# Probabilities of a decode attention transposed 128 rows at a time, and the softmax denominators of both batches formed in one step

## The chip, the cores and the metric

The kernel runs on one core of one Trainium2 chip. The metric is the device time of one execution in microseconds (us); lower is better. A ratio is the mean time of one kernel's runs over the mean of the other's in the same rounds, so it isn't quite the ratio of the medians that stand beside it.

## The reference

One decode step: 2 batches, 1 query token each, 32 heads of 128, a cache of 4096 positions, a gated mix with a small ReLU network.

```python
B, Sq, D = 2, 1, 512
Hq, Hkv, Sk, Dh = 32, 32, 4096, 128
q = (x @ wq).reshape(B, Sq, Hq, Dh).transpose(0, 2, 1, 3)
scores = jnp.einsum("bhqd,bhkd->bhqk", q, k_cache) * (Dh ** -0.5)
p = softmax(scores, axis=-1)
o = jnp.einsum("bhqk,bhkd->bhqd", p, v_cache)
a = o.transpose(0, 2, 1, 3).reshape(B, Sq, Hq * Dh) @ wo
b = jnp.maximum(B_x @ w1, 0) @ w2
g = sigmoid((x * gate_w).sum(-1, keepdims=True))
return g * a + (1 - g) * b            # all inputs bfloat16
```

The two caches are 64 blocks of 2 MB (32 of keys, 32 of values; a block is two heads of one batch). Together with the weights 145.43 MB have to be read.

## The kernel before

The instruction streams of the engines are built in program order, with named events between them. One queue (SP) issues all large loads, in order, into a ring of four buffers. A load waits until the block that used its buffer before has been consumed.

```python
for n in range(64):                      # 32 key blocks, then 32 value blocks
    waits = []
    if n >= NSLOT:                       # NSLOT = 4
        prev = n - NSLOT
        waits.append(f"T_{prev}_7" if prev < 32 else f"pv_{prev - 32}")
    load(f"ld_kv_{n}", kv_sb[:, n % NSLOT, :, :], kv_in(n), waits=waits, ...)
WO_CUTS = (0, 16, 24, 28, 30, 32)        # the output projection's weights, 4 MB, come last
for k in range(5): ...
```

So the load of value block 4 waits for `pv_0`, the end of the first block's product of probabilities and values (PV block 0). Between the scores and PV stands the softmax, one batch `g` after the other. A row of `E_sb[g]` is one of 4 groups of positions times 32 heads.

```python
def ptrans(g):                           # 64 transposes of 32 rows x 64 columns per batch
    for q in range(4):
        for k in range(16):
            ...
            src = E_sb[g][32 * q:32 * q + 32, col0:col0 + 64]
            P.add("pe", ... e.transpose(bank16(2 * g + b, 32 * blk, 32, 0, 64), src,
                        ident16[32*q:32*q+32, 32*q:32*q+32], tile_position=(32 * q, 0)), ...)

def denom_l(g):   # VectorE: lm[g] = jmask * l4[g]; waits for the exp of batch g
def denom(g):     # PE: ones @ lm[g], for g = 1 only after rg_0; VectorE: rinv, then rg
def stage_p(i):   # VectorE: two copies, the probabilities of block i out of PSUM into pst
def PV(p):        # PE: 64 matmuls with 2 moving columns; block i >= 2 waits for oT of block i - 2

for g in range(2):
    row_max(g); exps(g); ptrans(g)
for i in (0, 2, 1, 3):
    stage_p(i)
for g in range(2):
    denom_l(g); denom(g)
P.begin_loop(NIT)                        # 8 passes of 4 PV blocks
```

(Cuts are marked with dots, and bodies not needed for the argument are told in a comment. `l4` holds the sums of the exponentials that the exp leaves behind, one per row; `lm` spreads them so that a matmul with `ones` adds the four groups of a head; `rinv` is the reciprocal of that denominator, and `rg` is `rinv` times the gate.) Each engine takes its instructions in order, so PE reaches PV block 0 only after both batches' transposes and both denominator matmuls.

Of the kernel before, what the change touches and what calls it, by code (L numbers as in the profile page):

```python
# [4 lines left out]
ALU = mybir.AluOpType  # L5
# [9 lines left out]
PER = 4  # L15
# [120 lines left out]
def bass_gated_mix__gqa_block_cached__dense_activation_relu__decode_kernel(  # L136
# [12 lines left out]
    P = _Prog(nc)  # L149
# [3 lines left out]
    ident16 = sb("ident16", [128, 128], b16)  # L153
# [3 lines left out]
    ones = sb("ones", [128, 128], f32)  # L157
# [5 lines left out]
    g_sb = sb("g_sb", [128, 2], f32)  # L163
# [7 lines left out]
    kv_sb = sb("kv_sb", [128, NSLOT, 64, 128], b16)  # L171
# [3 lines left out]
    E_sb = [sb(f"E{g}", [128, 1024], b16) for g in range(2)]  # L175
    pst = sb("pst", [128, PER, 64, 2], b16)
# [5 lines left out]
    lm = sb("lm", [128, 2, 32], f32)  # L182
    rinv = sb("rinv", [128, 2, 32], f32)
    rg = sb("rg", [128, 2, 32], f32)
# [7 lines left out]
    PSB = PSF[:, :].bitcast(b16)  # L192

    def bank(b, c0, n, p0=0, p1=128):
        return PSF[p0:p1, 512 * b + c0:512 * b + c0 + n]

    def bank16(b, c0, n, p0=0, p1=128):
        return PSB[p0:p1, 1024 * b + c0:1024 * b + c0 + n]
# [8 lines left out]
    MISC, ACC = 7, 6  # L207
# [4 lines left out]
    def o_col(p):  # L212
        return bank(4 + p % 2, 256 + 2 * p, 2)

    def p_place(r):

        c = r // 8
        q = c % 4
        return q % 2, ((q // 2) * 2 + c // 4) * 8 + r % 8

    x_in = A_x.rearrange("b s d -> (b s) d")
    gw_in = gate_w.rearrange("(o d) -> o d", o=1)
# [22 lines left out]
    for n in range(64):  # L245
        waits = []
# [5 lines left out]
    for k in range(5):  # L252
# [7 lines left out]
          waits=["c_i0"], signal="c_id")  # L260
    P.add("pool", lambda e: e.memset(qmask[:], 0.0), signal="c_qm")
    P.add("pool", lambda e: e.memset(jmask[:], 0.0), signal="c_j0")
    for q in range(4):
# [3 lines left out]
              waits=[f"c_j{q}"], signal=f"c_j{q + 1}")  # L267
# [3 lines left out]
    for q in range(4):  # L271
        P.add("pool", lambda e, q=q: e.memset(dmask[32 * q:32 * q + 32, q:q + 1], 1.0), waits=["c_d0"] if q == 0 else [],
              signal="c_d" if q == 3 else None)
# [4 lines left out]
    for g in range(2):  # L278
        for c in range(8):
            P.add("pe", lambda e, g=g, c=c: e.matmul(S_chunk(g, c), lhsT=zt[:, 0:32], rhs=zt[:, :], start=True, stop=True,  # L280
                                                     tile_position=(0, 32 * (c % 4)), skip_group_check=True),
                  waits=["c_zt"] if c + g == 0 else [])
    for t in range(4):
        P.add("pe", lambda e, t=t: e.transpose(bank16(4, 2 * t, 2), x_sb[0:2, t:512:4], ident16[0:2, 0:2]),
              waits=["c_id", "ld_x"] if t == 0 else [], signal="xT" if t == 3 else None)
    for t in range(4):
        P.add("pe", lambda e, t=t: e.transpose(bank16(5, 2 * t, 1), gw_sb[0:1, t:512:4], ident16[0:1, 0:1]),  # L287
              waits=["ld_gw"] if t == 0 else [], signal="gwT" if t == 3 else None)
    P.add("dve", lambda e: e.tensor_copy(out=xT_sb[:, :, :], in_=bank16(4, 0, 8).rearrange("p (t b) -> p t b", t=4)),
          waits=["xT"], signal="xT_sb")  # L290
    P.add("dve", lambda e: e.tensor_copy(out=gwb_sb[:, :, :],
                                         in_=PSB[:, 5120:5128:2].unsqueeze(2).to_broadcast([128, 4, 128])),
          waits=["gwT"], signal="gwb")
    for t in range(4):
        P.add("pe", lambda e, t=t: e.matmul(bank(6, 0, 2), lhsT=gwb_sb[:, t, :], rhs=xT_sb[:, t, :],
                                            start=(t == 0), stop=(t == 3)),
              waits=["xT_sb", "gwb"] if t == 0 else [], signal="logit" if t == 3 else None)
    P.add("act", lambda e: e.activation(out=g_sb[:, :], in_=bank(6, 0, 2), func=ACT.Sigmoid), waits=["logit"], signal="g")
    P.add("dve", lambda e: e.tensor_scalar(out=gm_sb[:, :], in0=g_sb[:, :], scalar1=-1.0, scalar2=1.0, op0=ALU.mult, op1=ALU.add),
          waits=["g"], signal="gm")  # L300
    for h in range(HQ):
        for t in range(4):
            P.add("pe", lambda e, h=h, t=t: e.matmul(bank(7, 2 * h, 2), lhsT=wq_sb[:, t, h * 128:(h + 1) * 128],  # L303
                                                     rhs=xT_sb[:, t, :], start=(t == 0), stop=(t == 3)),
                  waits=["ld_wq"] if h + t == 0 else [], signal="qT" if h == HQ - 1 and t == 3 else None)
# [83 lines left out]
              waits=[f"negM_{g}"], signal=f"E_{g}")  # L389

    def ptrans(g):
        for q in range(4):
            for k in range(16):
                c = q + 4 * (k // 8)
                r = 8 * c + k % 8
                b, blk = p_place(r)
                col0 = (c // 4) * 512 + (k % 8) * 64
                src = E_sb[g][32 * q:32 * q + 32, col0:col0 + 64]
                P.add("pe", lambda e, q=q, b=b, blk=blk, src=src: e.transpose(  # L399
                    bank16(2 * g + b, 32 * blk, 32, 0, 64), src, ident16[32 * q:32 * q + 32, 32 * q:32 * q + 32], tile_position=(32 * q, 0)),  # L400
                    waits=[] if k else [f"pt_{g}_{q - 2}" if q > 1 else f"E_{g}"], signal=f"pt_{g}_{q}" if k == 15 else None)

    def denom_l(g):
        P.add("dve", lambda e: e.tensor_scalar(out=lm[:, g, :], in0=jmask[:, :], scalar1=l4[:, g:g + 1], scalar2=None, op0=ALU.mult),
              waits=[f"E_{g}", "c_j4"], signal=f"lm_{g}")

    def denom(g):
        P.add("pe", lambda e: e.matmul(bank(MISC, 32 * g, 32), lhsT=ones[:, :], rhs=lm[:, g, :], start=True, stop=True),  # L408
              waits=[f"lm_{g}", "c_one"] + (["rg_0"] if g else []), signal=f"lb_{g}")
        P.add("dve", lambda e: e.reciprocal(out=rinv[:, g, :], in_=bank(MISC, 32 * g, 32)), waits=[f"lb_{g}"], signal=f"rinv_{g}")  # L410
        P.add("dve", lambda e: e.tensor_scalar(out=rg[:, g, :], in0=rinv[:, g, :], scalar1=g_sb[:, g:g + 1], scalar2=None, op0=ALU.mult),
              waits=[f"rinv_{g}", "g"], signal=f"rg_{g}")


    def stage_p(i):
        hp, g = divmod(i, 2)
        p = i % PER
        for hh in range(2):
            base = PSB[0:64, 2048 * g:2048 * g + 2048].rearrange("p (b k j) -> p b k j", b=2, k=32)
            P.add("dve", lambda e, hh=hh, base=base: e.tensor_copy(  # L420
                out=pst[64 * hh:64 * hh + 64, p, :, hh].rearrange("p (b k) -> p b k", b=2), in_=base[:, :, :, 2 * hp + hh]),
                waits=[f"pt_{g}_2", f"pt_{g}_3", "c_ps"] + ([f"pv_{i - PER}"] if i >= PER else []),
                signal=f"pst_{i}" if hh else None, sem=f"ps{p}")

    def o_norm(i):
        hp, g = divmod(i, 2)
# [3 lines left out]

    def PV(p):
        for r in range(64):
            b, blk = p_place(r)

            def waits(t):
                i = PER * t + p
                return [f"ld_kv_{32 + i}", f"pst_{i}"] + ([f"oT_{i - 2}"] if i >= 2 else [])
            P.add("pe", lambda e, iv, r=r, k=32 * b + blk: e.matmul(o_col(p), lhsT=kv_sb[:, p, r, :], rhs=pst[:, p, k, :],  # L438
                                                                    start=(r == 0), stop=(r == 63)),
                  waits=waits if r == 0 else [], signal=(lambda t: f"pv_{PER * t + p}") if r == 63 else None)  # L440

# [59 lines left out]
    for g in range(2):  # L501
        row_max(g)
        exps(g)
        ptrans(g)
    for i in (0, 2, 1, 3):
        stage_p(i)
    for g in range(2):
        denom_l(g)
        denom(g)
    P.begin_loop(NIT)  # L510
    for p in range(PER):
        PV(p)
    P.end_loop()
    for i in range(32):
        o_norm(i)
        if i + PER < 32:
            stage_p(i + PER)
# [3 lines left out]
          waits=["proj"], signal="res")  # L521
    for b, eng in enumerate(("sp", "act")):
        P.add(eng, lambda e, b=b: e.dma_start(out_ap[b].rearrange("(c n) -> c n", c=4), out_sb[b:97 + b:32, :]), waits=["res"],
              signal=f"st_{b}", sem="st", inc=16)
# [51 lines left out]
```

## Time and profile before

| | before |
|---|---|
| time, median of the six runs of both rounds before and after the prediction | 354.77 us (354.48 to 354.87) |
| span of the profiled execution | 352.9 us |
| read from HBM, rate over the span | 145.43 MB, 412 GB/s |
| PE busy, VectorE busy | 68%, 38% of the span |
| chain that ended last (followed back from the last instruction, each time to what released it) | PE 51%, DMA 44% |

The shares of busy time point at PE, but they average two halves with different limits. These are two lines of the profile's page: the granted TensorE clock in tenths, and the rate of transfers, each in 40 equal slices of the span.

```profile
PEclk9999999999999999999996555555555555555555
...
GB/s 342 400 417 431 423 425 427 430 425 433 426 423 431 428 431 427 431 427 423 431 427 424 204 438 423 438 420 436 425 431 426 425 433 423 435 423 427 431 420 160
```

The rate is flat at about 428 GB/s in both halves, whether PE is busy or not, with one exception: the 23rd slice (194.1 to 202.9 us) has 204. That is the only place, besides start and tail, where the load queue was not working. The clock line shows that it falls to half one slice earlier (at 187.2 us, after the last score matmul has ended at 184.4) and stays there. Its first three digits stand before the first record of the clock (30.2 us) and show no measured value.

The next view is the windows view of that stretch: times, busy time of PE, its weight loads, VectorE, ScalarE and GpSimd with counts, the granted clock, the share of the 16 transfer engines that was busy, and their rate.

```profile
core 0: us, PE busy (x) PEld busy (x) DVE busy (x) ACT busy (x) POOL busy (x), PEclk, DMA share, GB/s
194.00:195.00 1.00, 0.31 (x2) 0.31 (x2) 0.59 (x3) 0.00 (x0) 0.00 (x0) 0.50 1.04 442
195.00:196.00 1.00, 0.32 (x2) 0.19 (x1) 0.60 (x3) 0.00 (x0) 0.00 (x0) 0.50 0.43 180
196.00:197.00 1.00, 0.80 (x15) 0.80 (x16) 0.27 (x2) 0.00 (x0) 0.00 (x0) 0.50 0.27 115
197.00:198.00 1.00, 1.00 (x43) 1.00 (x41) 0.47 (x2) 0.00 (x0) 0.00 (x0) 0.50 0.06 16
198.00:199.00 1.00, 1.00 (x44) 1.00 (x42) 0.43 (x3) 0.00 (x0) 0.00 (x0) 0.50 0.00 0
...
201.00:202.00 1.00, 1.00 (x43) 1.00 (x41) 0.03 (x1) 0.00 (x0) 0.00 (x0) 0.50 0.97 410
```

The last two columns matter: full until 195, a drain until 197, nothing from 198 to 199, full again after 201.

What ends the hole is in the timeline (start, duration, engine, line, operation, count, and in brackets the idle time just before and what ended it):

```profile
186.36 1.11 ACT L387 ACTIVATE E<-PS,negM 128x1024 bf16<-128x1024 f32 x1 [2.03 <-DVE negM L382]
...
187.62 5.76 PE L399 MATMUL PS<-ident,E 32*64 32x32 bf16 x128 [3.23 <-ACT E L387]
...
189.09 1.11 ACT L387 ACTIVATE E<-PS,negM 128x1024 bf16<-128x1024 f32 x1 [1.52 <-DVE negM L382]
...
193.41 0.95 DVE L420 COPY pst<-PS 64x64 bf16<-64x64 bf16 x4 [1.77 <-PE PS L399]
194.40 0.24 DVE L404 TENSOR_SCALAR lm<-jmask,l 128x32 f32<-128x32 f32 x1
...
194.69 0.63 PE L408 MATMUL PS<-lm,ones 128*128 128x32 f32 x2 [1.32 <-DVE lm L404]
...
195.91 0.23 DVE L404 TENSOR_SCALAR lm<-jmask,l 128x32 f32<-128x32 f32 x1
...
196.20 0.63 PE L408 MATMUL PS<-lm,ones 128*128 128x32 f32 x2 [0.87 <-DVE lm L404]
...
196.64 2.22 PE L438 MATMUL PS<-pst,kv_sb 128*128 128x2 bf16 x77
...
198.55 0.33 SPq L237 DMA_DIRECT2D kv_sb<-in_A_v_cache_dram  x1
```

Read it from the end. The load was issued at 198.55, when PV block 0 had ended; PV began at 196.64, behind the second denominator matmul (196.20), which waited for its `lm` on VectorE (195.91), which stood behind the first denominator's steps (from 194.40), which stood behind the copies, which waited for the 128 transposes (187.62 to 193.38). The exp of batch 1 was done by 190.29, and PE at that time was still at batch 0.

### The profile page before, as it was taken

How to read it: one execution, taken by the hardware profiler on the slowest of the kernel's cores; microseconds unless marked ns; L12 is line 12 of the kernel's file. 1: busy time of each engine (PE TensorE's matmuls, PEld its weight loads, DVE VectorE, ACT ScalarE, POOL GpSimd, SP SyncE). 2: the span in 40 equal slices, each digit the busy share in tenths (PEclk: the TensorE clock that was granted, in tenths of full speed). 3: DMA queues.
4: the chain of work that ended last, by engine and by line, in shares of the span. 5: the costliest groups of instructions: out<-in, count | busy, mean ns of one | idle time of the engine just before them, and what ended most of it. 6: DMA issues, size and time to landing. Idle time of an engine off the chain costs nothing.

```text
span 352.9 us, 11059 instructions
## 1 busy us (share of the span) xinstructions
PE 238.4 (68%) x5115; PEld 204.8 (58%) x5115; DVE 132.4 (38%) x294; ACT 99.5 (28%) x105; POOL 12.0 (3%) x52
## 2 busy tenths in 40 slices
PE   2539999999999999999986824433344333443244
PEld 0539878887878877887866824433344323443233
DVE  1005767666766666766675311001110011100010
ACT  1005665665656556565662000000000000000000
POOL 5000000000000000000000000000000000000000
PEclk9999999999999999999996555555555555555555
DMA  8999999999999999999999599999999999999994
GB/s 342 400 417 431 423 425 427 430 425 433 426 423 431 428 431 427 431 427 423 431 427 424 204 438 423 438 420 436 425 431 426 425 433 423 435 423 427 431 420 160
DMA packets 10515, 145.61 MB, mean 413 GB/s; under 512 B 1187, under 2 KB 1286, under 8 KB 1670
## 3 DMA queue, kind: packets, MB, share of 16 engines
q1 hardware_dynamic: 10488, 145.43, 97.4%
q8 instruction: 8, 0.13, 0.1%
q14 instruction: 5, 0.04, 0.0%
q10 hardware_dynamic: 14, 0.00, 0.0%
HBM read 145.43 MB, written 0.00 MB: 412 GB/s over the span
## 4 chain that ended last, share of the span: by engine, by line
PE 51%; DMA 44%; DVE 2%; SPq 1%; issue 1%; ACT 0%; DVEq 0%
PE PS L327 34%; DMA kv_sb<-in_A_v_cache_dram 30%; PE PS L338 10%; DMA wo_sb<-in_A_wo_dram 7%; DMA kv_sb<-in_A_k_cache_dram 7%; PE PS L438 5%; PE PS L399 2%; SPq L237 1%; DVE kt_sb L354 0%; PE PS L408 0%; ACT E L387 0%; DVE m L374 0%; DVE negM L382 0%; DVE pst L420 0%; DVE mq L377 0%
## 5 line engine op out<-in xcount | busy, mean ns | idle before, releaser
L327 PEld LDWEIGHTS PS<-ident,kv_sb 128*128 128x128 bf16 x2048 | 116.5, 99 | 19.2 <-issue 14.8
L327 PE MATMUL PS<-ident,kv_sb 128*128 128x128 bf16 x2048 | 123.6, 221 | 3.9 <-DMA kv_sb<-in_A_k_cache_dram 3.4
L354 DVE COPY kt_sb<-PS 128x1024 bf16<-128x1024 bf16 x160 | 105.4, 688 | 55.2 <-PE PS L327 55.2
L438 PE MATMUL PS<-pst,kv_sb 128*128 128x2 bf16 x2048 | 58.8, 165 | 86.3 <-DMA kv_sb<-in_A_v_cache_dram 86.3
L351 ACT ACTIVATE kt_sb<-PS 128x1024 bf16<-128x1024 bf16 x96 | 94.1, 1022 | 69.4 <-PE PS L327 69.3
L438 PEld LDWEIGHTS PS<-pst,kv_sb 128*128 128x128 bf16 x2048 | 57.1, 104 | 88.1 <-issue 65.7
L427 DVE TENSOR_TENSOR oT<-PS,rg 128x2 bf16<-128x2 f32 x32 | 5.1, 160 | 128.3 <-PE PS L438 128.3
L338 PE MATMUL PS<-kt_sb,qst 128*32 128x512 bf16 x512 | 38.3, 382 | 0.0
L338 PEld LDWEIGHTS PS<-kt_sb,qst 128*32 128x32 bf16 x512 | 13.3, 95 | 12.5 <-DVE kt_sb L354 3.6
L420 DVE COPY pst<-PS 64x64 bf16<-64x64 bf16 x64 | 14.4, 224 | 4.2 <-PE PS L399 3.4
L358 POOL COPY qst<-qmask 128x64 bf16<-128x64 bf16 x32 | 7.4, 237 | 151.6 <-PE PS L338 140.8
L399 PE MATMUL PS<-ident,E 32*64 32x32 bf16 x128 | 5.8, 210 | 3.2 <-ACT E L387 3.2
L399 PEld LDWEIGHTS PS<-ident,E 32*64 32x64 bf16 x128 | 5.7, 150 | 3.7 <-ACT E L387 3.7
L489 PE MATMUL PS<-wo_sb,os_sb 128*2 128x128 bf16 x128 | 4.3, 304 | 3.2 <-DMA wo_sb<-in_A_wo_dram 3.1
L303 PE MATMUL PS<-xT_sb,wq_sb 128*128 128x2 bf16 x128 | 3.6, 165 | 3.6 <-DMA wq_sb<-in_A_wq_dram 3.6
L303 PEld LDWEIGHTS PS<-xT_sb,wq_sb 128*128 128x128 bf16 x128 | 3.5, 104 | 3.7 <-DMA wq_sb<-in_A_wq_dram 3.7
L489 PEld LDWEIGHTS PS<-wo_sb,os_sb 128*2 128x2 bf16 x128 | 2.9, 112 | 4.4 <-DMA wo_sb<-in_A_wo_dram 2.2
L287 PE MATMUL PS<-ident,gw_sb 1*128 1x1 bf16 x4 | 0.3, 172 | 4.7 <-DMA gw_sb<-in_gate_w_dram 4.7
L387 ACT ACTIVATE E<-PS,negM 128x1024 bf16<-128x1024 f32 x2 | 2.2, 1113 | 3.6 <-DVE negM L382 3.6
L308 DVE TENSOR_SCALAR qmask<-PS 128x32 bf16<-128x32 f32 x2 | 0.5, 328 | 6.8 <-PE PS L303 6.8
L520 DVE TENSOR_TENSOR out_sb<-PS,f_sb 98x128 bf16<-98x128 f32 x1 | 0.3, 292 | 7.2 <-PE PS L489 7.2
L287 PEld LDWEIGHTS PS<-ident,gw_sb 1*128 1x128 bf16 x4 | 0.2, 114 | 4.8 <-DMA gw_sb<-in_gate_w_dram 4.8
(51 smaller groups left out, 32.0 us busy)
## 6 DMA issues: line engine op xcount, KB each, us to landing
kv_sb<-in_A_k_cache_dram SPq DMA_DIRECT2D x32, 2048.0 KB, 14.6
kv_sb<-in_A_v_cache_dram SPq DMA_DIRECT2D x32, 2048.0 KB, 17.6
wq_sb<-in_A_wq_dram SPq DMA_DIRECT2D x1, 4096.0 KB, 12.2
wo_sb<-in_A_wo_dram SPq DMA_DIRECT2D x1, 2048.0 KB, 22.1
w_sb<-in_B_w_dram SPq DMA_DIRECT2D x1, 1376.0 KB, 15.0
w_sb<-in_B_w_dram SPq DMA_DIRECT2D x1, 1280.0 KB, 19.3
wo_sb<-in_A_wo_dram SPq DMA_DIRECT2D x1, 1024.0 KB, 24.1
wo_sb<-in_A_wo_dram SPq DMA_DIRECT2D x1, 512.0 KB, 24.9
```

The costliest lines, as they stand in the source:

```text
L237: P.add(eng, lambda e: e.dma_start(dst, src), waits=waits, signal=name, sem=sem or name, inc=16)
L303: P.add("pe", lambda e, h=h, t=t: e.matmul(bank(7, 2 * h, 2), lhsT=wq_sb[:, t, h * 128:(h + 1) * 128], rhs=xT_sb[:, t, :], start=(t == 0), ...
L327: P.add("pe", lambda e, iv, q=q, rr=rr, r=r: e.transpose(bank16(4 + q % 4, rr * 128, 128), kv_sb[:, p, r, :], ident16[:, :]), waits=waits ...
L338: P.add("pe", lambda e, iv, c=c, hh=hh: e.matmul(S_chunk(p % 2, c), lhsT=qst[:, p, hh, :], rhs=kt_sb[:, p % NKT, 8 * c:8 * c + 8, 64 * hh: ...
L351: P.add("act", lambda e, dst=dst, src=src: e.activation(out=dst, in_=src, func=ACT.Copy), waits=w, signal=f"ev_{i}_{q}", sem=f"ev{p}{q}")
L354: P.add("dve", lambda e, dst=dst, src=src: e.tensor_copy(out=dst, in_=src), waits=w, signal=f"ev_{i}_{q}", sem=f"ev{p}{q}")
L358: P.add("pool", lambda e: e.tensor_copy(out=qst[:, p, :, :], in_=qmask[:, 32 * (i % 2) + i // 2 * 2:32 * (i % 2) + i // 2 * 2 + 2, :]), wa ...
L399: P.add("pe", lambda e, q=q, b=b, blk=blk, src=src: e.transpose(bank16(2 * g + b, 32 * blk, 32, 0, 64), src, ident16[32 * q:32 * q + 32, 3 ...
L420: P.add("dve", lambda e, hh=hh, base=base: e.tensor_copy(out=pst[64 * hh:64 * hh + 64, p, :, hh].rearrange("p (b k) -> p b k", b=2), in_=b ...
L427: P.add("dve", lambda e: e.tensor_tensor(out=oT[:, g, 2 * hp:2 * hp + 2], in0=o_col(i % PER), in1=rg[:, g, 2 * hp:2 * hp + 2], op=ALU.mult ...
L438: P.add("pe", lambda e, iv, r=r, k=32 * b + blk: e.matmul(o_col(p), lhsT=kv_sb[:, p, r, :], rhs=pst[:, p, k, :], start=(r == 0), stop=(r = ...
L489: P.add("pe", lambda e, r=r, c=c: e.matmul(acc(c), lhsT=os_sb[:, r, :], rhs=wo_sb[:, r, 128 * c:128 * c + 128], start=(r == 0), stop=(r == ...
```

## The change

Its intent: transpose all 128 rows of the probabilities in one matmul (32 matmuls instead of 128), form both denominators with one reciprocal, and put the `lm` steps early.

```diff
     def ptrans(g):
-        for q in range(4):
-            for k in range(16):
-                ...
-                P.add("pe", ... e.transpose(bank16(2 * g + b, 32 * blk, 32, 0, 64), src, ident16[32*q:..., 32*q:...], tile_position=(32 * q, 0)), ...)
+        for k in range(16):
+            P.add("pe", lambda e, k=k: e.transpose(PSB[0:64, 2048 * g + 128 * k:2048 * g + 128 * k + 128],
+                                                   E_sb[g][:, 64 * k:64 * k + 64], ident16[:, :]),
+                  waits=[] if k else [f"E_{g}"], signal=f"pt_{g}" if k == 15 else None)
...
-    def denom(g):
-        P.add("pe", ... lhsT=ones, rhs=lm[:, g, :] ..., waits=[f"lm_{g}", "c_one"] + (["rg_0"] if g else []), signal=f"lb_{g}")
-        P.add("dve", ... e.reciprocal(out=rinv[:, g, :], in_=bank(MISC, 32 * g, 32)), ...)
-        P.add("dve", ... rg[:, g, :] ...)
+    def denom():
+        for g in range(2):
+            P.add("pe", ... lhsT=ones, rhs=lm[:, g, :] ..., waits=[f"lm_{g}", "c_one"], signal="lb" if g else None)
+        P.add("dve", ... e.reciprocal(out=rinv[:, :, :], in_=bank(MISC, 0, 64)...), waits=["lb"], signal="rinv")
+        for g in range(2):
+            P.add("dve", ... rg[:, g, :] ..., waits=["rinv", "g"], signal=f"rg_{g}")
...
-    for i in (0, 2, 1, 3):
+    denom_l(0)
+    stage_p(0)
+    denom_l(1)
+    for i in (2, 1, 3):
         stage_p(i)
-    for g in range(2):
-        denom_l(g)
-        denom(g)
+    denom()
```

(Cut: the new order of columns in `p_place`, and the access patterns in `stage_p` and `PV` that follow from it.)

More of the change, by code (lines that the diff above doesn't have):

```diff
@@ L217, in p_place @@
         c = r // 8
-        q = c % 4
-        return q % 2, ((q // 2) * 2 + c // 4) * 8 + r % 8
+        return (c // 4 * 8 + r % 8) * 4 + c % 4
     x_in = A_x.rearrange("b s d -> (b s) d")
@@ L391, in ptrans @@
     def ptrans(g):
-        for q in range(4):
-            for k in range(16):
-                c = q + 4 * (k // 8)
-                r = 8 * c + k % 8
-                b, blk = p_place(r)
-                col0 = (c // 4) * 512 + (k % 8) * 64
-                src = E_sb[g][32 * q:32 * q + 32, col0:col0 + 64]
-                P.add("pe", lambda e, q=q, b=b, blk=blk, src=src: e.transpose(
-                    bank16(2 * g + b, 32 * blk, 32, 0, 64), src, ident16[32 * q:32 * q + 32, 32 * q:32 * q + 32], tile_position=(32 * q, 0)),
-                    waits=[] if k else [f"pt_{g}_{q - 2}" if q > 1 else f"E_{g}"], signal=f"pt_{g}_{q}" if k == 15 else None)
+        for k in range(16):
+            P.add("pe", lambda e, k=k: e.transpose(PSB[0:64, 2048 * g + 128 * k:2048 * g + 128 * k + 128],
+                                                   E_sb[g][:, 64 * k:64 * k + 64], ident16[:, :]),
+                  waits=[] if k else [f"E_{g}"], signal=f"pt_{g}" if k == 15 else None)
     def denom_l(g):
@@ L405, in denom_l @@
               waits=[f"E_{g}", "c_j4"], signal=f"lm_{g}")
-    def denom(g):
-        P.add("pe", lambda e: e.matmul(bank(MISC, 32 * g, 32), lhsT=ones[:, :], rhs=lm[:, g, :], start=True, stop=True),
-              waits=[f"lm_{g}", "c_one"] + (["rg_0"] if g else []), signal=f"lb_{g}")
-        P.add("dve", lambda e: e.reciprocal(out=rinv[:, g, :], in_=bank(MISC, 32 * g, 32)), waits=[f"lb_{g}"], signal=f"rinv_{g}")
-        P.add("dve", lambda e: e.tensor_scalar(out=rg[:, g, :], in0=rinv[:, g, :], scalar1=g_sb[:, g:g + 1], scalar2=None, op0=ALU.mult),
-              waits=[f"rinv_{g}", "g"], signal=f"rg_{g}")
+    def denom():
+        for g in range(2):
+            P.add("pe", lambda e, g=g: e.matmul(bank(MISC, 32 * g, 32), lhsT=ones[:, :], rhs=lm[:, g, :], start=True, stop=True),
+                  waits=[f"lm_{g}", "c_one"], signal="lb" if g else None)
+        P.add("dve", lambda e: e.reciprocal(out=rinv[:, :, :], in_=bank(MISC, 0, 64).rearrange("p (g j) -> p g j", g=2)),
+              waits=["lb"], signal="rinv")
+        for g in range(2):
+            P.add("dve", lambda e, g=g: e.tensor_scalar(out=rg[:, g, :], in0=rinv[:, g, :], scalar1=g_sb[:, g:g + 1], scalar2=None,
+                                                        op0=ALU.mult),
+                  waits=["rinv", "g"], signal=f"rg_{g}")
     def stage_p(i):
@@ L417, in stage_p @@
         p = i % PER
+        src = PSB[0:64, 2048 * g:2048 * g + 2048].rearrange("p (k j) -> p k j", j=32)
         for hh in range(2):
-            base = PSB[0:64, 2048 * g:2048 * g + 2048].rearrange("p (b k j) -> p b k j", b=2, k=32)
-            P.add("dve", lambda e, hh=hh, base=base: e.tensor_copy(
-                out=pst[64 * hh:64 * hh + 64, p, :, hh].rearrange("p (b k) -> p b k", b=2), in_=base[:, :, :, 2 * hp + hh]),
-                waits=[f"pt_{g}_2", f"pt_{g}_3", "c_ps"] + ([f"pv_{i - PER}"] if i >= PER else []),
-                signal=f"pst_{i}" if hh else None, sem=f"ps{p}")
+            P.add("dve", lambda e, hh=hh: e.tensor_copy(out=pst[64 * hh:64 * hh + 64, p, :, hh], in_=src[:, :, 2 * hp + hh]),
+                  waits=[f"pt_{g}", "c_ps"] + ([f"pv_{i - PER}"] if i >= PER else []),
+                  signal=f"pst_{i}" if hh else None, sem=f"ps{p}")
     def o_norm(i):
@@ L432, in PV @@
         for r in range(64):
-            b, blk = p_place(r)
             def waits(t):
@@ L437, in waits @@
                 return [f"ld_kv_{32 + i}", f"pst_{i}"] + ([f"oT_{i - 2}"] if i >= 2 else [])
-            P.add("pe", lambda e, iv, r=r, k=32 * b + blk: e.matmul(o_col(p), lhsT=kv_sb[:, p, r, :], rhs=pst[:, p, k, :],
+            P.add("pe", lambda e, iv, r=r, k=p_place(r): e.matmul(o_col(p), lhsT=kv_sb[:, p, r, :], rhs=pst[:, p, k, :],
                                                                     start=(r == 0), stop=(r == 63)),
```

## The prediction

> **What bounds the kernel now.** The load queue. It moves 145.43 MB; in the windows view the DMA share is 1.00 at 425 to 431 GB/s from 20 to 180 us and again from 220 to 340 us. Besides start and tail there is one hole, the single slice at 204 GB/s. All four buffers then hold value blocks not yet consumed, and the next load is issued only when PV block 0 ends (198.55). In fine windows the DMA share is 1.00 until 195.0, about 0.4 until 196.5, nothing from 198 to 199.5, full again from 201.5. Summed against 428 GB/s that is about 4.4 us of lost transfer. So only the time of that release matters.
>
> **Chain to it (chain of waits, timeline).** Last score 184.4, row maximum, exp of batch 0 done 187.6, 128 transposes of 32 rows on PE 187.62 to 193.39 (45 ns start to start, granted clock 0.50), copies of probabilities on DVE, then two denominators one after the other (194.40 to 196.6), PV from 196.64. The exp of batch 1 ends at 190.29, but PE is still busy with the first 64 transposes.
>
> **What the change does.** The same data goes in 32 matmuls of 128 moving columns. At clock 1.00 this trace shows 58 ns per 128-column transpose; at 0.50 I estimate 107 ns. The Trainium skill ("TensorE: Matmul & The Clock Gate", section "Wait — 56ns, not 53.3ns?") gives 106.7 ns for the cold array; the projection at the end of this trace agrees (four column tiles of 128 in about 117 ns). So 16 transposes take about 1.75 us, not 2.9. Batch 0's hide under the row maximum and exp of batch 1 (187.6 to 189.4, free until 190.29). Batch 1's run 190.35 to 192.1. Both lm steps move ahead under the transposes, and the second denominator matmul no longer waits for the first one's rg. One took 0.44 us before PV could start, so two about 0.85. PV starts at about 193.0 instead of 196.64. The remaining DVE work (two stage copies of 0.47, reciprocal 0.36, two rg of 0.24) fits before PV block 0 ends. POOL, ACT and the loads don't change.
>
> **Worth.** The load is issued 3.6 us earlier, at about 194.9, just as the previous loads drain. Everything after is bound by transfer, so this passes to the end nearly whole: 3.5 us of the 4.4 available. 354.66 - 3.5 = 351.2 us, range 350.4 to 352.4. That PE issues 96 matmuls fewer is worth nothing in itself. Chances: faster by over 2% 0.01 (the hole is 1.2% in all), within 2% 0.97, slower 0.02.
>
> **What would show each step.** Transposes about 107 ns apart; an idle gap on PE between the two batches' transposes, ended by the exp; PV from about 193.0; the load issued at about 194.9; no window of DMA share 0; the 204 GB/s slice rising to about 380 or more; PV spacing (4.9 us) unchanged later, so that the end shifts by the same amount.
>
> **What would make it wrong.** If the weight load of 64 columns doesn't overlap the matmul, a transpose takes about 160 ns, PV starts at 193.9, and the gain is 2.7 us. If the ramp-up of transfers (share 0.36 to 0.86 from 200 to 201.5) is paid again in full, it's nearer 3.3. If the drain overlaps better, up to 4.2. A slower PV with its probabilities strided by four would show as more than 1.86 us per block, and matter only in block 0.

## The result, and the profile after

| | before | after |
|---|---|---|
| time, median | 354.77 us (6 runs) | 351.13 us (350.82 to 352.24, 6 runs) |
| ratio | | 0.9904, 95% interval 0.9889 to 0.9918 |
| span of the profiled execution | 352.9 us | 349.2 us |
| HBM rate over the span | 412 GB/s | 416 GB/s |
| PE, VectorE instructions | 5115, 294 | 5019, 293 |
| load of value block 4 issued | 198.55 us | 195.03 us |

The interval is clear of 1. The same lines of the page:

```profile
PEclk9999999999999999999997555555555555555555
...
GB/s 338 405 415 428 430 424 422 434 428 424 425 435 426 423 430 434 428 424 434 430 424 423 381 422 439 426 422 430 434 428 421 432 430 428 424 435 428 424 420 167
```

The slice that had 204 GB/s has 381; all others are as before. The windows view of the same stretch:

```profile
194.00:195.00 1.00, 1.00 (x44) 1.00 (x42) 0.33 (x2) 0.00 (x0) 0.00 (x0) 0.50 0.99 410
195.00:196.00 1.00, 1.00 (x43) 1.00 (x41) 0.53 (x3) 0.00 (x0) 0.00 (x0) 0.50 0.60 229
196.00:197.00 1.00, 0.63 (x24) 0.54 (x21) 0.00 (x0) 0.00 (x0) 0.00 (x0) 0.50 1.04 295
197.00:198.00 1.00, 0.98 (x35) 0.98 (x36) 0.53 (x3) 0.00 (x0) 0.00 (x0) 0.50 0.78 279
198.00:199.00 1.00, 1.00 (x44) 1.00 (x42) 0.00 (x0) 0.00 (x0) 0.00 (x0) 0.50 1.15 492
```

The share never goes to zero, and by 198 the rate is full again. The timeline:

```profile
187.68 1.18 PE L392 MATMUL PS<-ident,E 128*64 128x128 bf16 x16 [3.24 <-ACT E L386]
...
189.15 0.24 DVE L397 TENSOR_SCALAR lm<-jmask,l 128x32 f32<-128x32 f32 x1
189.15 1.11 ACT L386 ACTIVATE E<-PS,negM 128x1024 bf16<-128x1024 f32 x1 [1.52 <-DVE negM L381]
...
190.39 0.24 DVE L397 TENSOR_SCALAR lm<-jmask,l 128x32 f32<-128x32 f32 x1 [0.63 <-ACT E L386]
...
190.41 1.91 PE L392 MATMUL PS<-ident,E 128*64 128x128 bf16 x16 [1.55 <-ACT E L386]
...
192.25 1.06 PE L402 MATMUL PS<-lm,ones 128*128 128x32 f32 x4
...
193.13 3.50 PE L433 MATMUL PS<-pst,kv_sb 128*128 128x2 bf16 x125
...
195.03 4.33 SPq L236 DMA_DIRECT2D kv_sb<-in_A_v_cache_dram  x3
...
197.02 3.58 PE L433 MATMUL PS<-pst,kv_sb 128*128 128x2 bf16 x127 [0.40 <-issue]
...
203.58 0.27 PE L433 MATMUL PS<-pst,kv_sb 128*128 128x2 bf16 x4 [2.98 <-issue]
```

The sixteen transposes of batch 0 end within the wait for batch 1's exp (PE then sits idle for 1.55 us, ended by ACT). Both `lm` steps are done before the transposes of batch 1 end. The denominator matmuls follow the transposes directly, PV starts at 193.13, and the load is issued at 195.03. The first row's 1.18 us and the fifth row's 1.91 us are the same work: in the first, the clock was still partly at 1.00 (0.83 on average from 187.6 to 189), in the second it was 0.50. The last two lines show something new, PV stopping twice within a block with no wait that the profile knows ("issue"); this is taken up below.

### The profile page after: what moved, and what is told of

Its sections match the earlier page's. It is cut to its first block, busy times and chain, and to the rows that moved or that the text cites. A ratio compares the mean times of both kernels' runs of the same rounds, so it can differ in the third digit from the quotient of the medians.

```text
span 349.2 us, 10866 instructions
## 1 busy us (share of the span) xinstructions
PE 236.4 (68%) x5019; PEld 202.6 (58%) x5019; DVE 132.0 (38%) x293; ACT 99.5 (28%) x105; POOL 12.0 (3%) x52
## 4 chain that ended last, share of the span: by engine, by line
PE 51%; DMA 43%; DVE 2%; issue 2%; SPq 1%; ACT 0%; DVEq 0%
PE PS L326 35%; DMA kv_sb<-in_A_v_cache_dram 29%; PE PS L337 10%; DMA wo_sb<-in_A_wo_dram 7%; DMA kv_sb<-in_A_k_cache_dram 7%; PE PS L433 5%; SPq L236 1%; DVE m L373 1%; PE PS L392 1%; DVE kt_sb L353 0%; ACT E L386 0%; DVE mq L376 0%; DVE negM L381 0%; PE PS L402 0%; PE PS L484 0%
## 5 line engine op out<-in xcount | busy, mean ns | idle before, releaser
L392 PE MATMUL PS<-ident,E 128*64 128x128 bf16 x32 | 3.1, 272 | 4.8 <-ACT E L386 4.8
L392 PEld LDWEIGHTS PS<-ident,E 128*64 128x64 bf16 x32 | 2.6, 142 | 5.5 <-ACT E L386 5.5
```

Source lines behind the costliest of these rows:

```text
L392: P.add("pe", lambda e, k=k: e.transpose(PSB[0:64, 2048 * g + 128 * k:2048 * g + 128 * k + 128], E_sb[g][:, 64 * k:64 * k + 64], ident16[: ...
```

## The experiments

**The theory.** Only the release counts: the kernel's time moves by the amount by which the load of value block 4 is issued earlier, until the hole is closed. **The rivals.** First, that the transposes are the gain and the denominators are tidying; second, that a removed transpose is worth the same wherever it stands; third, that the length of the chain through PE and VectorE is what is paid, and the hole in the transfers is only its shadow.

All kernels below gave correct results. The profiled executions are shifted against each other by up to 0.5 us, so releases are compared as the time from the start of the first transposes (which is the end of batch 0's exp) to the issue of the load. The gain is 1 minus the ratio, times the median of the kernel before in the same rounds.

| kernel | PE starts transposes | load issued | between | earlier by | time, median | ratio | gain |
|---|---|---|---|---|---|---|---|
| before | 187.62 | 198.55 | 10.93 | | 354.77 | | |
| after | 187.68 | 195.03 | 7.35 | 3.58 | 351.13 | 0.9904 | 3.4 |
| transposes alone | 188.08 | 197.90 | 9.82 | 1.11 | 353.91 | 0.9975 | 0.9 |
| denominators and order alone | 187.90 | 196.36 | 8.46 | 2.47 | 352.35 | 0.9934 | 2.3 |
| order of `lm` alone | 187.99 | 197.81 | 9.82 | 1.11 | 353.28 | 0.9966 | 1.2 |
| after, batch 0 the old way | 188.09 | 195.67 | 7.58 | 3.35 | 351.35 | 0.9908 | 3.3 |
| after, batch 1 the old way | 187.80 | 196.26 | 8.46 | 2.47 | 352.26 | 0.9935 | 2.3 |
| before, 1 MB of weights in the hole | 187.94 | 198.87 | 10.93 | 0 | 352.13 | 0.9933 | 2.4 |

Half the width of the 95% intervals is 0.0013 to 0.0017, or about 0.5 us.

### The transposes alone

The new `ptrans`, `p_place`, `stage_p` and `PV`; the denominators and their order as before.

```diff
     (ptrans, p_place, stage_p and PV as in the change)
-    denom_l(0); stage_p(0); denom_l(1); stage_p(2), (1), (3); denom()
+    for i in (0, 2, 1, 3):
+        stage_p(i)
+    for g in range(2):
+        denom_l(g); denom(g)
```

> The 128-row transposes alone, with the two denominators as they were before. Release theory (only the time at which PV block 0 frees its buffer counts): batch 1's transposes end at about 192.3 us, then the copies, then the two denominators in series, PV from about 195.6, the next load issued at about 197.4 instead of 198.55; gain 1.1 us, 353.6 us. Rival (the transposes are the change, the denominators are cosmetics): nearly the whole 3.6 us, 351.2 us.

Measured: 353.91 us (353.28 to 354.09), ratio 0.9975, interval 0.9962 to 0.9989. The timeline of this run:

```profile
190.81 1.91 PE L392 MATMUL PS<-ident,E 128*64 128x128 bf16 x16 [0.82 <-ACT E L386]
...
194.04 0.64 PE L401 MATMUL PS<-lm,ones 128*128 128x32 f32 x2 [1.32 <-DVE lm L397]
...
195.55 0.64 PE L401 MATMUL PS<-lm,ones 128*128 128x32 f32 x2 [0.87 <-DVE lm L397]
...
197.90 0.33 SPq L236 DMA_DIRECT2D kv_sb<-in_A_v_cache_dram  x1
```

The transposes end 1.1 us sooner, and then the two denominators take their 1.5 us one after the other as ever. The 32 matmuls are worth under a third of the gain; the rival that they are the change falls.

### The denominators and the order alone

```diff
     (ptrans, p_place, stage_p and PV as before)
+    denom() and the order of the change
```

> The denominators of both batches in one step and their new order on VectorE, with the 128 old transposes. Release theory: transposes end at 193.4 us as before, two denominator matmuls follow at once, PV from about 194.3, the load issued at about 196.1; gain 2.4 us, 352.4 us, the larger part of the change. If the first pass of the PV code has to be fetched while the loads are busy, a stall in PV block 0 may take up to 0.5 us of that. Rival (transposes are the change): under 0.5 us gained, 354.3 us or more.

Measured: 352.35 us (351.97 to 352.49), ratio 0.9934, interval 0.9920 to 0.9947. The timeline:

```profile
187.90 5.76 PE L399 MATMUL PS<-ident,E 32*64 32x32 bf16 x128 [3.24 <-ACT E L387]
...
193.59 1.06 PE L409 MATMUL PS<-lm,ones 128*128 128x32 f32 x4
...
196.36 0.33 SPq L237 DMA_DIRECT2D kv_sb<-in_A_v_cache_dram  x1
```

The denominator matmuls follow the last old transpose at once. No stall inside PV block 0 was seen. The release is 2.47 us earlier, and with the 1.11 us of the run before that makes 3.58 us, exactly what the whole change shows: the parts stand one behind the other on the same chain, so they add.

### Only the order of the lm steps

```diff
     (the kernel before)
-    for i in (0, 2, 1, 3):
-        stage_p(i)
-    for g in range(2):
-        denom_l(g); denom(g)
+    denom_l(0)
+    stage_p(0)
+    denom_l(1)
+    for i in (2, 1, 3):
+        stage_p(i)
+    for g in range(2):
+        denom(g)
```

> Only the order on VectorE: both lm steps early under the transposes, the old transposes, the two denominators still in series (the second matmul waits for the first one's rg). Release theory: the first denominator matmul at 193.4 us, its reciprocal behind the copies of batch 1 at about 194.4, second matmul at about 195.05, PV from 195.5, load issued at about 197.3; gain 1.1 to 1.2 us, 353.5 us. If the gain of the denominators is all in the joint step, nothing here: 354.7 us.

Measured: 353.28 us (353.27 to 353.61), ratio 0.9966, interval 0.9952 to 0.9979. The timeline:

```profile
187.99 5.76 PE L399 MATMUL PS<-ident,E 32*64 32x32 bf16 x128 [3.24 <-ACT E L387]
...
193.68 0.64 PE L408 MATMUL PS<-lm,ones 128*128 128x32 f32 x2
...
195.47 0.63 PE L408 MATMUL PS<-lm,ones 128*128 128x32 f32 x2 [1.15 <-DVE rg L411]
...
197.81 0.33 SPq L237 DMA_DIRECT2D kv_sb<-in_A_v_cache_dram  x1
```

Moving two VectorE instructions of 0.24 us forward, with every instruction kept, is worth 1.1 us of release: as much as replacing 128 transposes by 32. The joint step is the rest of the 2.47 us, 1.36, when it comes on top of the new order; alone it was not run. The third line says what it removes: the second denominator matmul still waits for `rg_0`. The shared reciprocal itself is not on the chain: in the changed kernel it starts at 193.35, after PV has begun at 193.13.

### Batch 0 the old way, batch 1 the old way

Two kernels, each the changed one with 64 small transposes for one batch and 16 large ones for the other. The column order of the probabilities follows the batch in `stage_p` and `PV`.

```diff
     (the changed kernel)
-        ptrans(g)
+        (ptrans_old if g == OLD else ptrans)(g)      # OLD = 0 in one kernel, 1 in the other
```

> The changed kernel, but batch 0 (not batch 1) transposed the old way, in 64 matmuls of 32 rows. Release theory: batch 0's transposes run while PE would wait for the exp of batch 1 (2.9 us of work in 2.7 us), so at most 0.2 us is lost against the changed kernel: 351.3 us. Rival (each transpose removed is worth the same, whichever batch it belongs to): half of the transposes' share is lost, 351.7 us, as in the run with batch 1 done the old way.

> The changed kernel, but batch 1 transposed the old way. Release theory: these 64 transposes stand between the exp of batch 1 and the denominators, 2.9 us instead of 1.75 us, so the whole share of the transposes is lost: load issued 1.1 us later than in the changed kernel, 352.3 us, as with all 128 old transposes and the new denominators (352.35 us). Rival (per transpose): 351.7 us.

Measured: batch 0 the old way 351.35 us (350.81 to 351.47), ratio 0.9908; batch 1 the old way 352.26 us (351.63 to 352.42), ratio 0.9935. The timeline with batch 0 the old way:

```profile
188.09 3.03 PE L404 MATMUL PS<-ident,E 32*64 32x32 bf16 x64 [3.24 <-ACT E L392]
...
191.04 1.92 PE L410 MATMUL PS<-ident,E 128*64 128x128 bf16 x16
...
195.67 0.33 SPq L242 DMA_DIRECT2D kv_sb<-in_A_v_cache_dram  x1
```

and with batch 1 the old way:

```profile
190.52 3.03 PE L404 MATMUL PS<-ident,E 32*64 32x32 bf16 x64 [1.65 <-ACT E L392]
...
196.26 0.33 SPq L242 DMA_DIRECT2D kv_sb<-in_A_v_cache_dram  x1
```

Each removes the same 48 matmuls from the 128. Taking them from batch 0 changes the release by 0.23 us, since that work fits almost wholly in PE's wait for the second exp; taking them from batch 1 is worth the whole 1.1 us, and with batch 1 the old way the release comes after 8.46 us, the same as with all 128 old transposes. The rival that each transpose has its price falls: nearly all of it is in the sixteen behind the last exp.

### Before, with 1 MB of weights in the hole

Nothing on the compute engines is changed. A quarter of the projection's weights, which have a place of their own, is loaded between value blocks 3 and 4.

```diff
+    WO_CUTS = (0, 8, 16, 24, 28, 30, 32)
     for n in range(64):
+        if n == 36:
+            load("ld_wo_0", wo_sb[:, 0:8, :], wo_in[:, 0:8, :])
         waits = []
 ...
-    WO_CUTS = (0, 16, 24, 28, 30, 32)
-    for k in range(5):
+    for k in range(1, 6):
```

> The kernel before, untouched on all compute engines; only 1 MB of the output projection's weights (8 of 32 rows), which needs no buffer to be freed, is loaded between value blocks 3 and 4 instead of at the end. Release theory: 2.45 us of the 4.4 us hole is filled with work that is needed anyway, PV still starts at 196.6 us and the load is still issued at 198.5 us, yet the kernel ends 2.4 us earlier, 352.3 us. Rival (the length of the chain through PE and VectorE is what is paid): no change, 354.7 us.

Measured: 352.13 us (351.98 to 352.59), ratio 0.9933, interval 0.9919 to 0.9946. The windows view of this run, columns as above:

```profile
195.00:196.00 1.00, 0.64 (x2) 0.50 (x2) 0.31 (x1) 0.00 (x0) 0.00 (x0) 0.50 0.86 360
...
197.00:198.00 1.00, 1.00 (x39) 1.00 (x40) 0.60 (x2) 0.00 (x0) 0.00 (x0) 0.50 0.85 352
198.00:199.00 1.00, 1.00 (x44) 1.00 (x42) 0.12 (x2) 0.00 (x0) 0.00 (x0) 0.50 0.47 188
```

The chain from exp to release is as long as before (10.93 us) and the kernel is 2.4 us faster, the time of 1 MB at the rate of the loads. So the chain is not what is paid. It is paid only as far as the queue runs dry. The third rival falls. (In this run the clock fell at 189.5 us, not at 187.2, so batch 0's 64 transposes took 2.05 us, PE then waited 0.68 us for the exp of batch 1, and the chain was no shorter: once more, batch 0's transposes are hidden.)

### After, with 0.5 MB and with 1 MB of weights in what is left of the hole

The same edit on the changed kernel, with 4 rows (0.5 MB) and with 8 rows (1 MB).

> The changed kernel, with 0.5 MB of the output projection's weights (4 of 32 rows, 1.2 us of transfer) loaded between value blocks 3 and 4. The windows of the changed kernel still show about 1.1 us of lost transfer between 194 and 202 us. Hole theory: 0.8 to 1.1 us of it is filled, 350.3 us. If what is left is not a lack of work for the loads but a cost of starting them, nothing changes: 351.1 us.

> The same with 1 MB (8 rows, 2.45 us of transfer). Hole theory: only about 1.1 us were left to fill, so it saturates: the same as with 0.5 MB within 0.2 us, 350.2 us, against a further 1.2 us (349.1 us) if more moved weights meant more gain whatever the hole. The tail is not touched, as the projection needs its first rows only some 3 us after the last value block landed.

Measured: 351.23 us (350.58 to 351.82), ratio 0.9910, with 0.5 MB; 350.79 us (350.48 to 350.89), ratio 0.9895, with 1 MB. The expected 0.8 to 1.1 us did not come. The windows view of the second shows that the hole itself is gone:

```profile
194.00:196.00 2.00, 2.00 (x81) 2.00 (x78) 0.92 (x6) 0.00 (x0) 0.00 (x0) 0.50 1.04 426
196.00:198.00 2.00, 1.50 (x56) 1.42 (x53) 0.48 (x3) 0.00 (x0) 0.00 (x0) 0.50 1.00 418
198.00:200.00 2.00, 2.00 (x81) 2.00 (x79) 0.57 (x4) 0.00 (x0) 0.00 (x0) 0.50 1.02 434
```

The share of the engines is an average. A load signals sixteen times, once for each transfer engine; the Trainium skill says so ("DMA: Bandwidth & Descriptors", section "Why a DMA increments its semaphore by 16 and not by 1": each participating engine adds one after its own data), and the trace agrees: every large load has sixteen completion marks. They don't name the engine, but the first and the last mark of a load show how far apart the engines are. While nothing interferes, marks of successive 2 MB blocks are 4.89 us apart.

```
first / last completion mark of the load, us
                            before           after            after + 1 MB
value block 3               195.62 / 197.87  195.60 / 197.74  195.67 / 197.96
weights moved (1 MB)        -                -                198.11 / 200.44
value block 4               205.33 / 207.56  202.01 / 203.88  203.00 / 205.33
last load of the kernel     347.49 / 349.75  344.12 / 346.10  342.74 / 345.98
```

From the rows of value blocks 3 and 4: an engine's pause was 205.33 - 195.62 - 4.89 = 4.8 us before and 202.01 - 195.60 - 4.89 = 1.5 us after (1.25 us by the last marks). With 1 MB moved there is no pause left (195.67 + 2.44 = 198.11, and 4.89 more is 203.00). So the hole was filled, and the first engine is indeed done 1.4 us earlier at the end. But the last engine is done only 0.1 us earlier, and the end waits for the last one. Its lag behind the first was 2.29 to 2.34 us from value block 3 up to the load with its first mark at 266.6 us, and 3.31 from the next one (271.5 us) on. With 0.5 MB moved it is the same picture: the first engine ends 1.0 us earlier than in the changed kernel (343.15), the last only 0.2 (345.92), and the lag steps from 2.05 to 2.66 us between the loads of 241.4 and 246.3 us.

### The changed kernel and the 1 MB kernel once more

> The changed kernel itself, unedited, beside the next one in the same rounds: 351.1 us, ratio to before 0.990. In the first profile its sixteen transfer engines ended 2.0 us apart.

> The kernel with 1 MB of projection weights in the hole once more. In its first profile the hole was closed on every transfer engine, and the first engine ended 1.4 us earlier than in the changed kernel, but the last only 0.1 us earlier, because its lag behind the first had grown from 2.3 to 3.3 us at about 270 us. If that lag is chance, this profile ends with a lag of about 2.3 us and a span about 1 us under that of the changed kernel (348.2 us), and the timed runs come out 0.5 to 1 us under it. If it belongs to this kernel, the lag is above 3 us again and the times are within 0.4 us of the changed kernel's.

Measured in the same rounds: 351.02 us (350.79 to 351.37), ratio 0.9901, and 350.77 us (350.53 to 351.05), ratio 0.9891. The lag of the last engine came again, from 2.40 to 3.35 us, between the loads with first marks at 266.7 and 271.6 us; in the changed kernel it stayed between 1.9 and 2.0 us from 226 us on. So it is not chance of one run. At 269.7 and 269.8 us the two traces have a packet of 8 KB on another queue, marked as instruction traffic; the changed kernel has one too (268.7 us) and no such step in its lag. In the run with 0.5 MB a packet of 16 KB, marked the same way, lies at its step (243.3 us). What makes one engine lose up to a microsecond there in one kernel and not in the other is not settled. The version with 1 MB moved is the fastest measured, by 0.25 to 0.35 us of the medians, and the intervals overlap: faster than the changed kernel is not shown.

## Why the prediction was right

Predicted 351.2 us, measured 351.13. Point by point:

- **What bounds it.** The load queue with one hole: shown by the run that filled half of it without touching the chain. The hole was put at 4.4 us from the mean share; by the completion marks it was a pause of 4.8 us on each engine. That term was undersized by a tenth, and it didn't matter, as the gain was set by the release.
- **Transposes at 107 ns.** Sixteen took 1.91 us including the modelled 0.31 us of the last, so (1.91 - 0.31) / 15 = 107 ns start to start at granted clock 0.50. (The prediction's 58 and 117 ns fit stretches divided by the count, with the modelled end of the last in them; from start to start the trace has 56 and 107.) The weight load did overlap. The 106.7 ns that the Trainium skill gives for the cold array ("TensorE: Matmul & The Clock Gate", "Wait — 56ns, not 53.3ns?") agrees with this trace.
- **Batch 0's transposes are hidden.** PE was idle for 1.55 us before batch 1's, ended by the exp, as said; and undoing them cost 0.23 us of release.
- **Two denominator matmuls in 0.85 us.** 193.13 - 192.25 = 0.88.
- **PV at 193.0, load at 194.9.** 193.13 and 195.03, in a trace shifted by 0.06. PV block 0 took 1.90 us, before 1.91, so the strided probabilities didn't slow it.
- **3.6 us earlier gives 3.5.** 3.58 us earlier gave 3.4 us by the ratio and 3.6 by the medians. The pause left on an engine is 1.25 to 1.5 us, so the release didn't yet run into the end of the hole.
- **That 96 fewer matmuls are worth nothing in themselves.** Shown by the two half kernels.
- **The slice at 380 or more; later spacing 4.9 us.** 381; 4.89.

What the prediction did not see: it never split the gain, though its numbers allowed it. The split is 1.1 us for the transposes, 1.1 for the order of two small VectorE steps, and 1.36 for the joint step on top of that order. And it didn't foresee that PV would now stop within blocks 1 and 3, for 0.40 and 2.98 us. The two stops are about 128 weight-load and matmul pairs apart (125 and then 127 matmuls are recorded before them, a few records being lost), that is 256 instructions, and at 194.6 and 201.4 us the trace has a 16 KB packet of instruction traffic that took 1.07 and 0.97 us among the loads; PE goes on 1.4 and 1.2 us after they end. That fits a wait for instruction fetch, which the Trainium skill describes ("Runtime: NRT & Kernel Launch", "Instruction fetch mechanics": 16 KiB blocks of 256 instructions); before, these packets came at 198.0 and 203.9 us, the first of them inside the hole, and no stop shows. No run was made to test it, but the kept traces fit: the stops come after 125 and 252 recorded matmuls in every trace with 32 transposes and the new denominators, and with batch 1 the old way, where 48 more transposes stand before PV, there is one stop, after 204, which is 48 fewer than 252. With batch 0 the old way, where the place is the same, the packet came at 196.1 us, some 3 us before PE was there, and there is no stop. So the stops sit at a place in PE's instruction stream; what PE waits for there is argued, not shown. It cost nothing, since three loads were issued by then and value block 4 landed at 203.88, when the stop was over.

## What to carry to other kernels

When the transfer rate is flat except for one dip, find the one event that issues the next load, and walk back from it; the price of every instruction is what it moves that event, and instructions in the shadow of another wait are free or nearly so. An instruction's place can be worth as much as its number: two steps of 0.24 us moved forward gained what 96 matmuls less did. And before work is moved to fill a hole, look at the slowest transfer engine and not at the mean: the end waits for that one.

## What the Trainium skill lacked or had wrong

- "TensorE: Matmul & The Clock Gate", "What's actually happening": full clock after one busy window of about 3.4 us. Here PE was busy from 196.64 to 203.63 us (kernel before, 2-column matmuls, 256 in 6.99 us) and the granted clock stayed at 0.50 to the end. Apart from its remark on transposes (next point), the page doesn't say which work counts as busy. In four of the twelve traces (order of `lm` alone, batch 0 the old way, before with 1 MB moved, the first of after with 1 MB moved) the clock went back to 1.00 for 3.41 us near the end, during the projection.
- The same page, "Part 4: PE-mode transpose": the full clock does not engage for transposes. In all twelve traces it did: the clock went to 1.00 between 28.7 and 31.6 us, in the middle of the first 80 transposes of key blocks (in the kernel before they run from 26.16 us, the clock rises at 30.20, and the first score matmul starts at 32.64), and the transposes were 107 ns apart before that moment and 56 ns after it. The trace lists them as matmuls with the identity.
- "Runtime: NRT & Kernel Launch", "Instruction fetch mechanics": crossing a 16 KiB boundary is called mostly hidden. With the loads at full rate the PE stopped 2.98 us at what looks like one (argued, not tested).
- "DMA: Bandwidth & Descriptors", "Where 436 GB/s comes from": it says that for HBM to SBUF the HBM side of about 358 GB/s binds. This single core read at 425 to 430 GB/s for 160 us on end, near the 435 GB/s that the page gives for the fabric. The page's section on measured bandwidth keeps the 358 for two cores that stream at once; the sentence on what binds leaves that out.
- "DMA: Bandwidth & Descriptors" says, in its section on the iDMA fabric, that a bulk load runs at the pace of its slowest engine, but I found no page that says how far the sixteen run apart (the page calls two of them usually slower, without a size): first and last completion of a load were 1.4 to 3.4 us apart from 24 us to the end (before, after, after with 1 MB moved), and the last one set the end.
